# Retention attention into an ELU block on one core: the VectorE side of the ELU, the last output tile and the last weight piece

## The chip, the cores and the metric

The kernel runs on one core of a Trainium2 chip. A core has TensorE (PE in the profile, with its weight loads as PEld), VectorE (DVE), ScalarE (ACT), GpSimd (POOL) and SyncE (SP, which here only issues DMAs). PE writes its results to PSUM, of which the kernel uses eight banks of 512 fp32 columns on 128 partitions; here DVE and ACT read and write PSUM and SBUF, and POOL works on SBUF. The metric is the device time of one execution in microseconds, the median of several runs.

## The reference

```python
scores = scale * np.matmul(q, k.transpose(0, 1, 3, 2))      # q, k, v: 8 batches, 8 heads, 576 positions, 64 wide
Dmat = np.where(rel >= 0, gamma[:, None, None] ** rel, 0.0) # rel = row - column, gamma per head
attn = np.matmul(scores * Dmat, v)
x = attn.transpose(0, 2, 1, 3).reshape(4608, 512)
h = x @ w_in                                                # w_in 512 x 2048
g = np.where(h > 0.0, h, np.exp(np.minimum(h, 0.0)) - 1.0)  # ELU
return g @ w_out                                            # w_out 2048 x 512, fp32
```

The decay `gamma ** (row - column)` splits into a factor for the row and one for the column, so that it can be put on q and k before the product. It is a linear attention with a decaying state.

## The kernel before, in words

The attention is cut into 40 units, five for each batch. Units 0 to 3 of a batch hold 256 positions and four heads each (0 and 1 the first 256 positions, 2 and 3 the next); the fifth, the tail (u = 4, 9, 14, ...), holds the last 64 positions for all heads. For a unit, q, k and v are loaded (step `ld`, on SP's queue), cast to bf16 with the decay factors (`ca`, on POOL, DVE or ACT), transposed (by PE with `tr` and a copy `tc` for units 0 to 7, by a DMA transpose `dt` on SP's queue from unit 8 on), and then PE makes the scores (`sc`), DVE multiplies them with the causal mask (`mk`, L469), PE makes the inner product with v (`va`), the part from the state (`in`) and the state's update (`st`); DVE adds up the state (`pm`, `pe`), DVE or POOL put it in block-diagonal form (`dm`, `de`), and ACT or DVE copy the result to the bf16 tile `xt` (`ou`, L215).

The tokens then go through the two products in nine groups of 512. `f` is the first product for one of the 16 slices of 128 hidden columns (four matmuls of 512 columns, tile `ph`, a PSUM bank). Groups 0 and 1 are cut in two token segments, 256 and 256, 320 and 192, so that the first segment can begin before the second is there. The ELU takes three steps for each `f`: `ex` (L621, ACT: e = exp(ph), fp32 in SBUF), `re` (the side), `el` (the join, DVE, bf16 tile `g`). The side has two forms. On ACT (L627) it is relu(ph) written back over ph in PSUM, and the join is min(e - 1, ph) (L640). On DVE (L631) it is em = min(e - 1, e), a bf16 tile in SBUF made from e alone, and the join is min(max(ph, 0), em) (L642). `a` is a quarter of the second product for 128 tokens (four matmuls of 512 columns, L207, tile `pm`), `y` its copy to SBUF (L215, ACT or DVE), `so` its store (L661, on POOL's queue, for the last four tiles on SP's).

The weights come in four pieces of w_in (`wi.0` to `wi.3`) and four of w_out (`wo.0` to `wo.3`), 512 KB each, on POOL's queue (L295). Quarter m of `a` needs `wo.m` alone.

What each engine does, and in which order, is written out in the string `PLAN` (1559 steps, L23 to L155): the steps are issued in that order, and each engine keeps it for its own. A step with `>` has a gate: `ld.10.q>wo.3` doesn't issue its load until the piece wo.3 has landed, and everything behind it in SP's queue waits too. `wm.8.x1` is eight matmuls on zeros that are thrown away; they keep PE at work while the first loads arrive. PSUM is shared out by bank: h0, h1, h2 and pm, x0 and x1 go round among `f`, `a`, transposes and the attention's results, and the scores have two banks.

The step order around the change, before: POOL's queue issues wi.1, then wi.0, wi.2, wi.3, wo.0, wo.1, wo.2; units 5 and 6 have their k loaded ahead of the weights, all other loads from unit 4 on are behind gates; wo.3 is issued after POOL's cast `ca.5.q.p`. At the end the tiles 8.1, 8.2 and 8.3 of the last group are finished first, and 8.0 last: `a.8.0.3`, then `y.8.0.v` and `so.8.0.y` for 128 tokens by 512 columns.

Of the kernel before, what the change touches and what calls it, by code (L numbers as in the profile page):

```python
# [9 lines left out]
FP32 = mybir.dt.float32  # L10
# [13 lines left out]
ld.1.k ld.0.q wm.8.x1 ld.0.v k0 ld.2.q ld.3.q.1 ld.0.k ca.1.k.p ld.3.v.1 wm.3.h0 ld.1.q ca.0.q.v ld.3.q.0 wm.8.h2  # L24
ld.3.k.1 ld.3.k.0 ld.1.v ld.2.k ca.2.q.p tr.1.k.x0 ld.3.v.0 tr.0.q.x1 tc.1.k.v wm.3.h1 ld.2.v ca.0.k.v wm.6.x0 ld.5.k
ca.0.v.v ld.6.k tc.0.q.v ca.1.q.v wm.2.h2 tr.0.k.h0 st.0 tc.0.k.v ca.3.q.v.1 ca.3.k.p.0 sc.0 pm.0 tr.2.q.x0 pe.0
dm.0.p mk.0 tr.1.q.h2 wm.7.h1 ca.1.v.p tc.1.q.s wi.1 tc.2.q.v ca.2.k.v ca.3.q.p.0 va.0 ca.3.k.v.1 st.1 sc.1 pm.1
tr.3.1.h1 pe.1 in.0 dm.1.p mk.1 tr.3.0.pm ou.0.1.s tr.2.k.h0 wi.0 tc.2.k.s wm.1.x1 ou.0.0.v wi.2 tc.3.0.s in.1
tc.3.1.v sc.2 ca.2.v.s va.1 ca.3.v.v.0 de.0.p wm.2.h1 mk.2 ca.3.v.s.1 ou.1.1.s wi.3 ou.1.0.s st.3.0 st.2 wo.0 pm.2
sc.3.1 st.3.1 sc.3.0 wm.3.x1 mk.3.1 dm.2.p wo.1 mk.3.0 va.2 in.2 pm.3 wo.2 pe.2 ou.2.0.s dm.3.v va.3.0  # L30
f.0.4.0.256.2.h2 ou.2.1.s de.1.v k1 va.3.1 in.3.0 in.3.1 f.0.0.0.256.2.pm ou.3.0.v.0 ou.3.1.s.1 ou.3.1.v.0 ex.0.4.0
ou.3.0.v.1 pe.3 f.0.6.256.256.2.x1 re.0.4.0.s de.3.p ex.0.0.0 el.0.4.0 f.0.6.0.256.2.x0 ex.0.6.256 f.0.11.0.512.1.h2
re.0.6.256.v ex.0.6.0 el.0.6.256 re.0.6.0.s f.0.8.0.512.1.h0 ex.0.11.0 ca.6.k.v f.0.10.0.512.1.h1 re.0.11.0.s el.0.6.0
ex.0.8.0 f.0.4.256.256.2.x1 el.0.11.0 ex.0.10.0 re.0.8.0.v f.0.2.0.256.2.x0 re.0.0.0.s ex.0.4.256 el.0.8.0
f.0.13.0.512.1.h2 ex.0.2.0 el.0.0.0 re.0.4.256.s f.0.0.256.256.2.h0 re.0.10.0.s el.0.4.256 re.0.2.0.s
# [123 lines left out]
def kernel(  # L159
# [9 lines left out]
    nc = tc.nc  # L169
# [543 lines left out]
```

## Time and profile before

| | |
|---|---|
| median of 5 runs | 316.09 us (315.61 to 317.82) |
| the profiled execution | 315.61 us, span 313.9 us, so 1.71 us lie outside the span |
| granted PE clock | 1.00 |
| PE, DVE, ACT, POOL busy | 302.6, 229.6, 174.3, 132.7 us |
| HBM read, written | 36.70 MB, 9.44 MB |
| ELU sides on ACT, on DVE | 110, 42 |

The profile is of one execution. A busy PE includes the fill of its pipeline, so the gaps that it shows are real ones, and some small waits are hidden within busy time. Where durations are given for an operation, they are of one instruction. Idle time of an engine is listed with what ended it.

### The profile page before, as it was taken

To read this page: it belongs to the slowest core of one execution; us is meant where nothing else is said; L and a number is where in the kernel's file an instruction comes from. 1 tells how busy PE (TensorE), PEld (TensorE's weight loads), DVE (VectorE), ACT (ScalarE), POOL (GpSimd) and SP (SyncE) were. 2 spreads that over 40 slices of the span, in tenths; PEclk is the share of its full clock that TensorE was granted. 3 is DMA by queue.
4 is the path that set the end of the run, shared out by engine and by line. 5 is a ranking of instruction groups with operands and counts; after the bars stand their busy time and mean duration, and the time that the engine had idled before them with its cause. 6 is when DMAs were issued, how large, how long until landed. Compare 5 with 4: busy or idle time off the path is not lost.

```text
span 313.9 us, 7897 instructions
## 1 busy us (share of the span) xinstructions
PE 302.6 (96%) x3143; PEld 155.6 (50%) x3143; DVE 229.6 (73%) x435; ACT 174.3 (56%) x365; POOL 132.7 (42%) x196
## 2 busy tenths in 40 slices
PE   8999998999999989999998999999999999999995
PEld 3557554567555444444544454445444444444442
DVE  2888867997879957759899787898966585653512
ACT  2049946587258577563865556645636576745200
POOL 5480174666778455282695469522002120000100
PEclk9999999999999999999999999999999999999999
DMA  7999999999998999999699996121200010001034
GB/s 203 267 190 200 190 245 225 243 229 225 261 219 203 231 272 243 225 246 258 176 241 277 268 173 134 34 73 63 52 21 33 37 67 2 0 25 44 0 115 153
DMA packets 101140, 49.92 MB, mean 159 GB/s; under 512 B 45296, under 2 KB 98544, under 8 KB 101104
## 3 DMA queue, kind: packets, MB, share of 16 engines
q1 hardware_dynamic: 94320, 36.84, 53.8%
q0 software_dynamic: 6784, 12.59, 16.3%
q8 instruction: 24, 0.39, 0.5%
q14 instruction: 12, 0.10, 0.1%
HBM read 36.70 MB, written 9.44 MB: 147 GB/s over the span
## 4 chain that ended last, share of the span: by engine, by line
PE 76%; DMA 10%; DVE 7%; POOL 2%; SPq 2%; issue 1%; ACT 1%; ACTq 0%; DVEq 0%
PE pm L207 35%; PE ph L207 31%; DMA w_out<-in_moe_w_out_dram 7%; PE x L207 5%; PE warm L207 3%; DVE em L631 2%; PE sc L207 2%; DMA rvt<-in_v_dram 2%; DMA rqk<-in_q_dram 1%; DVE pt L469 1%; SPq L383 1%; DVE g L640 1%; POOL w_in L295 1%; DVE g L642 1%; ACT e L621 1%
## 5 line engine op out<-in xcount | busy, mean ns | idle before, releaser
L207 PE MATMUL ph<-xt,w_in 128*128 128x512 bf16 (+3 forms) x672 | 142.0, 349 | 2.7 <-DVE g L642 1.6
L207 PE MATMUL pm<-w_out,g 128*128 128x512 bf16 x576 | 142.9, 379 | 0.8 <-DMA w_out<-in_moe_w_out_dram 0.8
L621 ACT ACTIVATE e<-ph 128x512 f32<-128x512 f32 (+2 forms) x152 | 86.8, 575 | 78.3 <-PE ph L207 74.2
L207 PEld LDWEIGHTS <-w_in 128*128 128x128 bf16 x672 | 63.1, 98 | 60.8 <-issue 3.4
L640 DVE SCALAR_TENSOR_TENSOR g<-e,ph 128x512 bf16<-128x512 f32 (+3 forms) x123 | 71.0, 596 | 27.5 <-ACT ph L627 26.2
L207 PEld LDWEIGHTS <-g 128*128 128x128 bf16 x576 | 54.6, 98 | 62.0 <-issue 1.4
L627 ACT ACTIVATE ph<-ph 128x512 f32<-128x512 f32 (+2 forms) x110 | 62.4, 573 | 0.0
L661 POOL DMA_DIRECT2D out_dram<-ot x32 | 18.2, 570 | 85.6 <-DVE ot L215 54.6
L631 DVE SCALAR_TENSOR_TENSOR em<-e 128x512 bf16<-128x512 f32 (+2 forms) x42 | 37.1, 885 | 14.4 <-ACT e L621 14.1
L469 DVE TENSOR_TENSOR pt<-sc,mask 128x1024 bf16<-128x1024 f32 x31 | 37.7, 1215 | 0.7 <-PE sc L207 0.6
L367 POOL TENSOR_TENSOR qkn<-rqk,gq 128x512 bf16<-128x512 f32 (+1 forms) x26 | 28.0, 1075 | 14.5 <-DMA rqk<-in_q_dram 11.7
L367 POOL TENSOR_TENSOR qkn<-rqk,gk 128x512 bf16<-128x512 f32 (+1 forms) x24 | 25.2, 1050 | 13.6 <-DMA rqk<-in_k_dram 10.1
L215 ACT CAST xt<-x 128x256 bf16<-128x256 f32 (+1 forms) x59 | 19.9, 388 | 17.6 <-PE x L207 15.9
L642 DVE SCALAR_TENSOR_TENSOR g<-ph,em 128x512 bf16<-128x512 f32 (+3 forms) x45 | 28.1, 631 | 1.1
L566 POOL TENSOR_TENSOR s_mid<-mid,diag 128x256 bf16<-128x256 f32 x26 | 17.6, 678 | 19.3 <-DVE mid L557 10.9
L215 ACT COPY ot<-pm 128x512 f32<-128x512 f32 x22 | 12.9, 589 | 18.2 <-PE pm L207 18.1
L566 POOL TENSOR_TENSOR s_end<-end,diag 128x256 bf16<-128x256 f32 x25 | 15.8, 638 | 14.9 <-DVE end L563 14.9
L215 DVE COPY ot<-pm 128x512 f32<-128x512 f32 x14 | 9.5, 687 | 13.1 <-PE pm L207 13.1
L215 DVE CAST xt<-x 128x256 bf16<-128x256 f32 (+1 forms) x31 | 11.6, 387 | 7.6 <-PE x L207 5.0
L362 POOL TENSOR_TENSOR qkt<-rqt,gq 128x256 bf16<-128x256 f32 x13 | 9.0, 701 | 16.0 <-DMA rqt<-in_q_dram 13.2
L215 POOL CAST vn<-rv 128x512 bf16<-128x512 f32 x18 | 11.2, 624 | 9.8 <-PE x L207 6.2
L207 PE MATMUL warm<-zero 128*128 128x512 bf16 x43 | 13.1, 459 | 1.3 <-DVE zero L220 1.3
(64 smaller groups left out, 185.0 us busy)
## 6 DMA issues: line engine op xcount, KB each, us to landing
out_dram<-ot POOLq DMA_DIRECT2D x32, 256.0 KB, 3.2
rqk<-in_k_dram SPq DMA_DIRECT2D x31, 256.0 KB, 5.2
rqk<-in_q_dram SPq DMA_DIRECT2D x31, 256.0 KB, 4.9
rv<-in_v_dram SPq DMA_DIRECT2D x31, 256.0 KB, 4.3
w_in<-in_moe_w_in_dram POOLq DMA_DIRECT2D x4, 512.0 KB, 7.0
w_out<-in_moe_w_out_dram POOLq DMA_DIRECT2D x4, 512.0 KB, 11.9
rqt<-in_k_dram SPq DMA_DIRECT2D x8, 128.0 KB, 4.8
rqt<-in_q_dram SPq DMA_DIRECT2D x8, 128.0 KB, 4.1
```

The costliest lines, as they stand in the source:

```text
L207: return pin(nc.tensor.matmul(*a, **kw))
L215: return pin(nc.scalar.copy(dst, src) if eng == "s" else engines[eng].tensor_copy(dst, src))
L362: return pin(engines[eng].tensor_tensor(dst[:, hs], src[:, hs], g, ALU.mult))
L367: return pin(engines[eng].tensor_tensor(to, x, g, ALU.mult))
L469: return pin(nc.vector.tensor_tensor(ptt[u].rearrange("p h i n -> p i h n"), sc.rearrange("p i (h n) -> p i h n", h=2), m.unsqueeze(1).to_ ...
L566: return pin(engines[eng].tensor_tensor(dst.rearrange("p h (j d) -> p h j d", j=2), src.unsqueeze(2).to_broadcast([P, 2, 2, D]), diag.unsq ...
L621: return pin(nc.scalar.activation(e[:, : n * nf], ph[:, : n * nf], AF.Exp))
L627: return pin(nc.scalar.activation(ph[:, : n * nf], ph[:, : n * nf], AF.Relu))
L631: return pin(nc.vector.scalar_tensor_tensor(em[:, : n * nf], e, -1.0, e, ALU.add, ALU.min))
L640: last = pin(nc.vector.scalar_tensor_tensor(dst, more[0][:, c], -1.0, ph[:, c], ALU.add, ALU.min))
L642: last = pin(nc.vector.scalar_tensor_tensor(dst, ph[:, c], 0.0, more[1][:, c], ALU.max, ALU.min))
L661: return pin({"p": nc.gpsimd, "y": nc.sync}[eng].dma_start(out[i0 : i0 + P, :], ots.pop((int(g), int(it)))))
```

## The change

Three edits in the Python, and a new `PLAN`.

1. The side of the ELU on DVE is relu(ph), written back over ph in PSUM, as it was on ACT. The tile em is gone, and there is one form of the join.
2. The output tile 8.0 is made in two halves of 256 columns, each with 16 matmuls into a PSUM bank of its own (h1 and x1), a copy of its own (the first on ACT, the second on DVE) and a store of its own on SP's queue.
3. `wo.3` is issued with the other weight pieces, ahead of the loads that have gates. The pieces go out as wi.1, wi.2, wi.3, wi.0, wo.1, wo.2, wo.0, wo.3. The first load with a gate is `ld.5.q>wo.0`.

The plan is another one throughout (1556 steps, none of its first steps in the old place). It holds the same work of PE but for the halves and the zero matmuls (43 before, 38 after). Which engine does a step changes as follows:

| steps | before | after |
|---|---|---|
| ELU side, ACT / DVE | 110 / 42 | 88 / 64 |
| casts of q and k, POOL / DVE | 63 / 19 | 68 / 14 |
| casts of v, POOL / ACT / DVE | 23 / 12 / 6 | 17 / 23 / 1 |
| block-diagonal states, POOL / DVE | 51 / 13 | 56 / 8 |
| copies to xt, ACT / DVE | 52 / 30 | 48 / 34 |
| copies of transposes, ACT / DVE | 6 / 9 | 7 / 8 |
| copies of output tiles, ACT / DVE | 22 / 14 | 19 and a half tile / 16 and a half tile |

```diff
 PLAN = """
-ld.1.k ld.0.q wm.8.x1 ld.0.v k0 ld.2.q ld.3.q.1 ld.0.k ca.1.k.p ld.3.v.1 wm.3.h0 ld.1.q ca.0.q.v ld.3.q.0 wm.8.h2
-ld.3.k.1 ld.3.k.0 ld.1.v ld.2.k ca.2.q.p tr.1.k.x0 ld.3.v.0 tr.0.q.x1 tc.1.k.v wm.3.h1 ld.2.v ca.0.k.v wm.6.x0 ld.5.k
...
-sc.3.1 st.3.1 sc.3.0 wm.3.x1 mk.3.1 dm.2.p wo.1 mk.3.0 va.2 in.2 pm.3 wo.2 pe.2 ou.2.0.s dm.3.v va.3.0
-f.0.4.0.256.2.h2 ou.2.1.s de.1.v k1 va.3.1 in.3.0 in.3.1 f.0.0.0.256.2.pm ou.3.0.v.0 ou.3.1.s.1 ou.3.1.v.0 ex.0.4.0
...
-f.0.12.0.512.1.pm el.0.10.0 ex.0.13.0 el.0.2.0 f.0.14.0.512.1.h1 re.0.13.0.s ex.0.0.256 el.0.13.0 ld.4.k>wo.1
...
-re.0.2.256.s ld.7.k>wi.3 el.0.12.0 ca.5.v.p ld.4.v>wi.2 a.0.1.1 el.0.2.256 ex.0.15.0 ca.5.q.p re.0.15.0.s a.0.0.2
-ld.7.v>wo.0 ca.6.v.s wo.3 el.0.15.0 tr.4.q.pm ld.9.k>wi.1 tr.5.q.x1 tc.4.q.v a.0.1.2 ca.7.q.p ld.8.q tc.5.q.s
...
-a.8.2.0.h2 a.8.1.3 a.8.2.1 y.8.1.v so.8.1.y a.7.3.3 a.8.2.2 y.7.3.v a.8.3.2 so.7.3.p a.8.2.3 a.8.3.3 y.8.2.v so.8.2.y
-a.8.0.3 y.8.3.s so.8.3.y y.8.0.v so.8.0.y
+ld.0.k ld.0.q wm.7.x1 ld.1.q k0 ld.1.k ld.6.k ld.3.v.0 ca.0.k.p ld.0.v ld.2.k tr.0.k.h1 wm.6.x0 ld.2.q ld.1.v ld.3.q.0
+ld.3.k.0 wm.7.h2 ca.1.k.v ld.2.v ca.1.q.v ld.3.v.1 ca.0.q.v ld.3.k.1 wm.4.h0 ld.3.q.1 tc.0.k.v ca.0.v.p ld.5.k
+tr.0.q.pm tr.1.k.x0 tr.1.q.h0 ca.2.k.v wm.4.h2 tc.0.q.v tr.2.k.x1 ca.2.q.p sc.0 st.0 mk.0 wm.7.h1 ca.1.v.s tc.2.k.s
+ca.3.q.p.0 pm.0 wi.1 tc.1.k.v tr.2.q.pm pe.0 va.0 ca.2.v.s tc.2.q.v ca.3.k.p.0 st.1 tc.1.q.s dm.0.p pm.1 ca.3.v.s.1
+wi.2 pe.1 sc.1 in.0 mk.1 wm.3.h2 dm.1.p ou.0.0.s ou.0.1.s ca.3.k.p.1 st.2 sc.2 ca.3.q.p.1 pm.2 tr.3.0.h0 mk.2 in.1
+wi.3 tc.3.0.s va.1 tr.3.1.pm ca.3.v.s.0 wi.0 ou.1.1.s st.3.1 tc.3.1.v ou.1.0.v sc.3.1 de.0.p st.3.0 sc.3.0 va.2 mk.3.1
+f.0.6.0.256.2.pm dm.2.p pm.3 de.1.p mk.3.0 in.2 ex.0.6.0 dm.3.p pe.2 ou.2.1.v va.3.0 ou.2.0.s wo.1 in.3.0 in.3.1
+ou.3.1.v.0 va.3.1 wo.2 ou.3.0.v.0 f.0.4.0.256.2.h2 ou.3.0.v.1 ou.3.1.v.1 pe.3 ca.5.k.p f.0.4.256.256.2.x1 ex.0.4.0
+re.0.6.0.s k1 re.0.4.0.v f.0.11.0.512.1.x0 ex.0.4.256 wo.0 el.0.4.0 f.0.6.256.256.2.h0 ex.0.11.0 ca.6.k.p el.0.6.0
+f.0.14.0.512.1.h1 ex.0.6.256 re.0.4.256.v de.2.p re.0.11.0.s f.0.10.0.512.1.pm el.0.4.256 ex.0.14.0 de.3.p
+f.0.8.0.512.1.h2 el.0.11.0 wo.3 ex.0.10.0 re.0.6.256.v re.0.14.0.s f.0.2.256.256.2.x1 ex.0.8.0 el.0.14.0 re.0.10.0.s
+el.0.6.256 f.0.0.0.256.2.h1 ex.0.2.256 el.0.10.0 re.0.8.0.s ex.0.0.0 el.0.8.0 f.0.2.0.256.2.pm re.0.0.0.s
+f.0.0.256.256.2.h2 el.0.0.0 ex.0.2.0 tr.6.k.h0 re.0.2.0.v ex.0.0.256 f.0.9.0.512.1.x0 el.0.2.0 re.0.0.256.s
+f.0.15.0.512.1.h1 ex.0.9.0 tc.6.k.v re.0.2.256.v f.0.12.0.512.1.pm el.0.2.256 ld.5.q>wo.0 a.0.0.0.h0 el.0.0.256
+ex.0.15.0 re.0.15.0.s ex.0.12.0 ld.4.k>wo.0 tr.5.k.x1 re.0.9.0.v a.0.1.0.h2 ld.4.q>wi.1 tc.5.k.v ld.6.q>wi.2 el.0.15.0
+f.0.13.0.512.1.x1 ld.5.v>wo.2 el.0.9.0 a.0.1.1 ld.7.k>wo.0 re.0.12.0.v ex.0.13.0 ld.4.v re.0.13.0.v a.0.0.1 ca.5.q.p
+el.0.12.0 a.0.1.2 ld.6.v>wo.3 ca.4.q.v ca.4.k.p ld.7.v>wo.0 a.0.0.2 el.0.13.0 ld.7.q>wi.1 ca.6.q.v tr.5.q.x0 tr.4.q.h1
+ld.8.v>wo.1 tc.5.q.s a.0.1.3 ca.5.v.p ld.9.k>wo.2 tc.4.q.s tr.6.q.pm ld.9.q>wo.2 y.0.1.v st.5 ca.4.v.p ca.7.k.p sc.4
+sc.5 ld.8.q>wo.1 pm.5 a.0.0.3 mk.4 ld.10.k>wi.0 pe.5 mk.5 a.0.3.0.h2 dm.5.p ld.8.k>wi.3 ca.6.v.s ld.10.q>wo.3 y.0.0.s
...
+so.7.2.p a.8.3.2 a.7.3.1 a.8.1.3 a.8.2.2 y.8.1.v so.8.1.y a.8.3.3 a.7.3.2 y.8.3.s a.8.2.3 so.8.3.y a.7.3.3 y.8.2.v
+so.8.2.y b.8.0.0.h1 y.7.3.v so.7.3.p b.8.0.1.x1 yb.8.0.0.s sb.8.0.0.y yb.8.0.1.v sb.8.0.1.y
 """
...
-        ph, n, nf, more = es[int(g), int(ft), int(lo)]
+        ph, n, nf, e = es[int(g), int(ft), int(lo)]
         if eng == "s":
             return pin(nc.scalar.activation(ph[:, : n * nf], ph[:, : n * nf], AF.Relu))
-        em = epool.tile([P, TG], BF16, name="em", tag="em")
-        more.append(em)
-        e = more[0][:, : n * nf]
-        return pin(nc.vector.scalar_tensor_tensor(em[:, : n * nf], e, -1.0, e, ALU.add, ALU.min))
+        return pin(nc.vector.tensor_scalar_max(ph[:, : n * nf], ph[:, : n * nf], 0.0))
...
-            if len(more) == 1:
-                last = pin(nc.vector.scalar_tensor_tensor(dst, more[0][:, c], -1.0, ph[:, c], ALU.add, ALU.min))
-            else:
-                last = pin(nc.vector.scalar_tensor_tensor(dst, ph[:, c], 0.0, more[1][:, c], ALU.max, ALU.min))
+            last = pin(nc.vector.scalar_tensor_tensor(dst, e[:, c], -1.0, ph[:, c], ALU.add, ALU.min))
...
+    def ffn2_columns(g, it, c, tag):
+        g, it, c = int(g), int(it), int(c)
+        accs[g, it, c] = bank(tag, "pm")
+        for ft in range(NFT):
+            last = mm(accs[g, it, c][:, : DM // 2], gts[g, ft][:, it * P : (it + 1) * P],
+                      w_sb["o"][ft // 4][:, ft % 4, c * DM // 2 : (c + 1) * DM // 2],
+                      start=(ft == 0), stop=(ft == NFT - 1))
+        return last
+
+    def out_y_columns(g, it, c, eng):
+        g, it, c = int(g), int(it), int(c)
+        ots[g, it, c] = opool.tile([P, DM // 2], FP32, name="oc", tag="oc", bufs=2)
+        return copy(eng, ots[g, it, c], accs[g, it, c][:, : DM // 2])
+
+    def store_columns(g, it, c, eng):
+        g, it, c = int(g), int(it), int(c)
+        i0 = g * TG + it * P
+        return pin({"p": nc.gpsimd, "y": nc.sync}[eng].dma_start(
+            out[i0 : i0 + P, c * DM // 2 : (c + 1) * DM // 2], ots.pop((g, it, c))))
```

## The prediction

> **What bounds the kernel now.** I read the page's busy times first, then the busy time in stretches of 10 us, then the chain of work that ended last, and for the operations that the change touches the groups by shape and the timeline.
>
> ```profile
> PE 302.6 (96%) x3143; PEld 155.6 (50%) x3143; DVE 229.6 (73%) x435; ACT 174.3 (56%) x365; POOL 132.7 (42%) x196
> PEclk9999999999999999999999999999999999999999
> ```
>
> PE is busy for 302.64 of 313.9 us at a clock of 1.00, so the change can only move the 11.26 us in which PE stands still, or PE's work in the start. Where they lie (columns: stretch, length, then PE, PEld, DVE, ACT, POOL busy, clock, DMA share, GB/s):
>
> ```profile
> 0.00:10.00 10.00, 8.75 (x34) 3.71 (x35) 3.50 (x24) 2.01 (x4) 4.70 (x19) 1.00 0.83 222
> 10.00:20.00 10.00, 8.92 (x205) 5.33 (x204) 9.18 (x19) 3.59 (x8) 7.56 (x11) 1.00 1.12 223
> ...
> 40.00:50.00 10.00, 9.18 (x151) 5.10 (x149) 6.67 (x15) 4.48 (x11) 5.57 (x7) 1.00 1.18 246
> 50.00:60.00 10.00, 9.31 (x139) 5.48 (x138) 8.76 (x15) 6.50 (x17) 6.32 (x9) 1.00 0.95 211
> 60.00:70.00 10.00, 9.58 (x180) 6.33 (x179) 9.78 (x23) 7.42 (x22) 7.12 (x9) 1.00 1.19 242
> ...
> 110.00:120.00 10.00, 8.55 (x99) 4.25 (x97) 6.19 (x11) 8.52 (x20) 5.47 (x7) 1.00 1.18 277
> ...
> 160.00:170.00 10.00, 8.42 (x85) 3.95 (x84) 9.93 (x12) 4.85 (x11) 8.36 (x12) 1.00 1.15 250
> ```
>
> Start 2.33 us; then 0.82 + 0.69 + 0.42 + 1.45 + 1.58, with 0.04 in 20-30 and 0.21 in 200-210: 5.21 us; and 3.73 us after PE's last matmul ends at 310.17. The chain says what the 0.82 us at 48 us waits for:
>
> ```profile
> 21.66 14.57 DMA w_out<-in_moe_w_out_dram
> 36.25 4.19 DMA rqk<-in_q_dram
> 40.52 0.99 POOL qkn L367
> 41.51 7.17 DMA w_out<-in_moe_w_out_dram
> 48.72 1.89 PE pm L207 x8
> ```
>
> The seventh weight piece lands at 36.23, a gated load of q behind it at 40.4, POOL casts it, and only then issues wo.3, for which PE waits until 48.72. For 160-170, the timeline:
>
> ```profile
> 162.99 0.62 POOL L215 CAST vn<-rv 128x512 bf16<-128x512 f32 x1
> 163.26 3.90 DVE L631 SCALAR_TENSOR_TENSOR em<-e 128x512 bf16<-128x512 f32 x1
> 163.57 1.05 POOL L367 TENSOR_TENSOR qkn<-rqk,gk 128x512 bf16<-128x512 f32 x1
> 164.57 1.05 POOL L367 TENSOR_TENSOR qkn<-rqk,gq 128x512 bf16<-128x512 f32 x1
> 165.57 1.04 POOL L367 TENSOR_TENSOR qkn<-rqk,gk 128x512 bf16<-128x512 f32 x1
> ...
> 168.02 1.02 PE L207 MATMUL ph<-xt,w_in 128*128 128x512 bf16 x4 [1.20 <-DVE g L642]
> ```
>
> One em took 3.90 us beside four POOL casts in a row, and ended 0.55 us after the last of them; its join came late, and PE had no free bank. The prices, by shape:
>
> ```profile
> L631 DVE SCALAR_TENSOR_TENSOR em<-e 128x512 bf16<-128x512 f32 x37 | 32.7, 884 | 14.4 <-ACT e L621 14.1
> L642 DVE SCALAR_TENSOR_TENSOR g<-ph,em 128x512 bf16<-128x512 f32 x36 | 24.6, 687 | 0.9
> L215 DVE COPY ot<-pm 128x512 f32<-128x512 f32 x14 | 9.5, 687 | 13.1 <-PE pm L207 13.1
> L627 ACT ACTIVATE ph<-ph 128x512 f32<-128x512 f32 x91 | 54.1, 599 | 0.0
> ```
>
> **The change, part by part.** The sum is made against the profiled execution: span 313.9, time 315.61, so 1.71 outside. It is the fastest of five; the median is 0.48 higher, which I add at the end.
>
> *The ELU side.* Removed: 42 em, 37.2 us of DVE. Added: 64 relus in PSUM, which the trace doesn't show on DVE. From below the nearest is the DVE copy out of PSUM in bf16 (0.42 for 512), from above the mean em with its waits (0.88). I take 0.687, the DVE copy of the same 512 fp32 columns out of PSUM, because only the place of the result differs, and on ACT that place costs nothing (in place 0.599, exp into SBUF 0.598). The joins keep their price (0.681 with e, 0.687 with em). 57 x 0.687, 4 of 320 columns x 0.475 and 3 of 384 x 0.54 are 42.7 us. With what else moves on DVE (10 casts x 0.68 less, 5 states x 0.42 less, one transpose copy x 0.42 less, 4 copies to xt x 0.44 and 2.5 output copies x 0.69 more) its total changes by 42.7 - 37.2 - 6.8 - 2.1 - 0.4 + 1.8 + 1.7 = -0.3 us: DVE stays near 229 us. ACT loses 22 relus and gains 11 casts (-13.0 + 6.8) and falls below 170. Both are work beside PE. On the path is only the waiting: the 1.58 us of 160-170 and the 0.21 us of 200-210, where the chain also runs through an em (1.49 us at 203.29), go: -1.8. Neither wait is added to: the relu waits for exp as em did, with the same join queued behind it on DVE.
>
> The Trainium skill (SBUF - State Buffer, section "SBUF: two separate sides") says that a DVE instruction with two SBUF inputs and a GpSimd instruction take turns on a port pair, each holding it whole. The 3.90 us em agrees. By that rule the 15 casts left on DVE can still be held up, the relus can't, and the sum would be the same -1.8. Against the change speaks VectorE: DVE Perf Modes, section on the TRN2 errata: 120 cycles of fixed cost for a PSUM source against 58 for SBUF. By that the sum would lose an estimated 64 x 62 cycles / 0.96 GHz = 4.1 us of DVE work; the rows 0.687 (PSUM) and 0.692 (median em) show no such difference.
>
> *The last tile.* PE does the same: a 256-column matmul in the first product takes 7.8 us / 64 = 122 ns, a 512-column one 119.2 / 480 = 248. The last copy is 256 columns wide: 0.41 as the join of that width, for 0.69: -0.28. The store is 128 KB instead of 256: the DMA moves up to 410 GB/s there, so -0.32 us of the 2.0 us from issue to landing; bounds 0 (all of it fixed) and -0.65. The first half's copy and store and the extra issue on SP lie beside the second half's 16 matmuls (about 1.9 us). Sum -0.6, between -0.3 and -0.9.
>
> *Weights and the start.* Loads: 17 before the weights in both plans, about 0.9 us each 256 KB. Walking the new order with the rows' durations: POOL casts q of unit 3 at 12.3 and issues wi.1 at 13.05 (13.57 before); mask 1 runs 15.1-16.3, mask 2 16.75-17.95, mask 3 from 19.0, each held by the two score banks; the first `f` starts at 19.4 (21.81 before), but the second must wait for unit 3's states, which are now all on POOL behind wi.3 and wi.0: 22.2, against 23.26. So the start gains 1.05. Then 13 more `f` of 0.866 and a transpose bring PE to `a.0.0.0` at 34.6. That needs wo.0, now the seventh piece, and the seventh landed at 36.2; 0.2 earlier with wi.1: a new wait of 1.4. In its place before, PE was at this step at 35.77. The start's gain is gone: +0.2.
>
> Behind that gate stands all of SP's queue: units 4 to 8 start loading at 36.0, not 33.42, and wo.3's 512 KB run ahead of them (2.5 us at the 205 GB/s of 20-40 us). v of unit 6 lands near 46.5, ACT casts it (0.62), and `st.6`, which PE reaches at 46.4, waits some 0.7; the 0.82 us for wo.3 are gone. Going on, PE begins group 1 at 52.1 (52.22 before): -0.1 for all of it. k of unit 8 has 3968 KB ahead and with it: 55.4 at 205 GB/s, 53.3 at 230 (the page shows 225 and 245 there). Cast 1.04, transpose 1.3 and 4.1 to land: 61.8 or 59.7, and PE wants its scores near 59: between 0 and 2.8; I take +0.6. Early part +0.5, bounds -1.9 (the start's gain and the 0.82 kept) and +4.
>
> *The order elsewhere.* The 1.45 us at 112 are v of unit 19: issued at 104.58, landed at 110.28, cast on ACT. Between its load and its use lie 6.0 us of PE work in the old plan, 20.7 in the new one: gone. New waits of the kind have to be reckoned with; the loads nearest to their use in the new plan are v of units 5 and 6 (5.0, 4.8 us, counted above), 9 (5.6) and 36 (5.4, when the DMA is nearly idle); and DVE has up to 11.7 us of work for 10 us of PE around 50-60 (11.2 before). I take +1.0 for them, between 0 and 4.
>
> Sum: -1.8 - 0.6 + 0.5 - 1.45 + 1.0 = -2.35. Span 311.55, run 313.26, median 313.7.
>
> **The rivals.** *No change:* the plan trades waits for waits; gaps after the start come to about 5 us again. For it: DVE's total is the same, and the start's gain meets the weights. Against: em's hold-ups (9 us over undisturbed ones: 37 x 0.192 and 3 x 0.64) can't return. Only the tail stays: 315.5.
>
> *Starved early, about no change or slower:* the 2.6 us of the gate and the 2.5 us of wo.3 reach PE whole, in 45-62 us: 5.1 - 0.1 instead of +0.5. -2.35 + 4.5 = +2.1: 318.2. It is slower once the early part comes to more than 4.5 us. For it: v of units 5 and 6 stand within 5 us of their use. Against: four quarters `a.0.2` can fill, and in the old plan SP stood at its gate from 45.0 to 48.7 and doesn't now.
>
> *DVE becomes the bound, slower:* the relu costs the upper price: 64 x 0.19 = 12.2 us more on DVE, which is over 0.78 busy in most stretches up to 230 us; half of it reaches PE: -2.35 + 6.1: 319.8. It decides from 0.81 us a relu (64 x 0.124 / 2 = 3.95). For it: no row shows this operation. Against: the DVE copy at 0.687.
>
> **How the numbers follow.** About 0.5%, 1.6 us, is what a measurement of this kernel can tell from no change. Forecast 0.47, all of it faster; no change 0.20, same; starved 0.17, half same and half slower; DVE bound 0.16, slower. So faster 0.47, same 0.28, slower 0.25. The forecast's own range is 311.0 to 314.5. For 8 in 10 the lower end is the early part at -1.9 with the tail's -0.9: 310.9; the upper end goes between the two slower cases, 319.0.
>
> **What would show it.** Right: no em, relus near 0.69 us with hardly any spread; PE full in 160-170 and 110-120; a wait for w_out at `a.0.0.0` near 36 us and none at 48; 3.1 us after the last matmul. Wrong: relus above 0.8, or PE waiting for x, sc or DMA rows between 45 and 70 by more than 4 us; a start that gains 2 us and keeps it would make it better than forecast.

## The result and the profile after

The changed kernel takes 315.32 us (median; 312.63 to 318.05) beside 316.46 us for the kernel before in the same comparison: a ratio of 0.9983, with a 95% interval from 0.9967 to 0.9999. That is 0.5 us, and less than the 0.5% that this kernel's measurement can tell from no change. Forecast were 313.7 us and a gain of 0.74%. This ratio and those below leave out disturbed executions, which took over 1.5% more than the fastest of their kernel (24 of the 80 of before, 2 of the 43 of the changed kernel); that is why it isn't the ratio of the two medians.

The profiled execution took 313.78 us with a span of 312.1, 1.8 us under the profiled one of before, near the forecast's -2.35. It flatters the kernel: it is 1.5 us under its own median, where before's was 0.5 us under the median of its first five runs.

The page of the changed kernel, busy times (us, share of the span, instructions):

```profile
PE 300.9 (96%) x3154; PEld 156.4 (50%) x3154; DVE 226.5 (73%) x449; ACT 167.3 (54%) x348; POOL 131.2 (42%) x200
```

DVE is 3 us lower than before (229.6) and ACT 7 us (174.3). The busy time in stretches of 10 us (stretch, length, then PE, PEld, DVE, ACT, POOL busy, clock, DMA share, GB/s):

```profile
0.00:10.00 10.00, 7.59 (x35) 3.04 (x36) 3.56 (x24) 2.01 (x4) 3.75 (x19) 1.00 0.83 219
...
40.00:50.00 10.00, 9.95 (x157) 5.69 (x154) 7.63 (x16) 3.48 (x8) 6.36 (x9) 1.00 1.26 244
...
80.00:90.00 10.00, 7.67 (x135) 4.43 (x133) 4.26 (x12) 3.71 (x9) 7.47 (x11) 1.00 1.19 241
...
110.00:120.00 10.00, 10.00 (x81) 4.74 (x79) 8.24 (x17) 6.61 (x14) 5.96 (x7) 1.00 1.05 242
...
160.00:170.00 10.00, 10.00 (x140) 4.96 (x138) 7.24 (x14) 5.64 (x14) 8.43 (x12) 1.00 0.95 202
```

The waits of before at 48, 112 and 165 us are gone. But in all PE stands still for 11.1 us, and it was 11.3 before: new are 2.33 us at 80-90, 1.2 us more in 0-10 (2.41 for 1.25) and 0.9 us more in 20-40. What makes this span shorter is PE's work, 300.9 us for 302.6: the zero matmuls take 10.0 us and not 12.6. So waits were traded for waits, and the 1.8 us of this profile are not those of the forecast's sum. The groups by shape:

```profile
L635 DVE SCALAR_TENSOR_TENSOR g<-e,ph 128x512 bf16<-128x512 f32 x120 | 80.3, 682 | 17.3 <-ACT ph L626 15.5
L627 DVE TENSOR_SCALAR ph<-ph 128x512 f32<-128x512 f32 x57 | 39.7, 696 | 21.1 <-ACT e L620 20.7
```

A relu takes 0.696 us; the longest of all 64 took 0.700. The timeline shows the new wait:

```profile
78.41 1.26 SPq L383 DMA_TRANSPOSE qkT<-qkt  x1
...
82.05 1.14 ACT L215 CAST vn<-rv 128x512 bf16<-128x512 f32 x2 [0.88 <-DMA rv<-in_v_dram]
...
82.71 0.32 PE L207 MATMUL x<-vn,qkn 64*64 64x64 bf16 x16 [0.64 <-ACT vn L215]
...
84.95 0.26 PE L207 MATMUL x<-qkT 64*64 64x64 bf16 x8 [1.69 <-DMA qkT<-qkt]
```

v of unit 13 was issued at 77.07 and lands about 82, when PE already wants it; the transposing DMA of unit 14, issued at 78.41, is there at 84.9. In before these were issued at 73.1 and 75.0, with their uses at the same place (82 us).

### The profile page after: what moved, and what is told of

Its sections match the earlier page's. It is cut to its first block, busy times and chain, and to the rows that moved or that the text cites. A ratio compares the mean times of both kernels' runs of the same rounds, so it can differ in the third digit from the quotient of the medians.

```text
span 312.1 us, 7915 instructions
## 1 busy us (share of the span) xinstructions
PE 300.9 (96%) x3154; PEld 156.4 (50%) x3154; DVE 226.5 (73%) x449; ACT 167.3 (54%) x348; POOL 131.2 (42%) x200
## 4 chain that ended last, share of the span: by engine, by line
PE 77%; DMA 14%; POOL 4%; SPq 3%; issue 1%; DVE 1%; POOLq 0%; DVEq 0%
PE pm L207 36%; PE ph L207 33%; PE x L207 5%; DMA w_out<-in_moe_w_out_dram 4%; DMA qkT<-qkn 3%; SPq L332 2%; PE sc L207 2%; DMA qkT<-qkt 2%; DMA out_dram<-ot 2%; DMA rqk<-in_q_dram 2%; DMA rqt<-in_q_dram 1%; POOL qkn L367 1%; POOL w_in L295 1%; POOL s_mid L566 1%; POOL w_out L295 0%
## 5 line engine op out<-in xcount | busy, mean ns | idle before, releaser
L207 PE MATMUL pm<-w_out,g 128*128 128x512 bf16 (+1 forms) x592 | 143.3, 373 | 0.1
L635 DVE SCALAR_TENSOR_TENSOR g<-e,ph 128x512 bf16<-128x512 f32 (+3 forms) x168 | 97.8, 605 | 18.8 <-ACT ph L626 16.5
L627 DVE TENSOR_SCALAR ph<-ph 128x512 f32<-128x512 f32 (+2 forms) x64 | 43.2, 676 | 22.0 <-ACT e L620 21.6
L626 ACT ACTIVATE ph<-ph 128x512 f32<-128x512 f32 (+2 forms) x88 | 49.5, 570 | 0.0
L367 POOL TENSOR_TENSOR qkn<-rqk,gk 128x512 bf16<-128x512 f32 (+1 forms) x27 | 27.3, 1013 | 16.3 <-DMA rqk<-in_k_dram 15.2
L215 DVE COPY ot<-pm 128x512 f32<-128x512 f32 x16 | 11.0, 689 | 15.1 <-PE pm L207 12.6
L215 ACT COPY ot<-pm 128x512 f32<-128x512 f32 x19 | 11.1, 586 | 16.3 <-PE pm L207 16.1
L215 ACT CAST vn<-rv 128x512 bf16<-128x512 f32 (+1 forms) x18 | 10.5, 593 | 15.0 <-DMA rv<-in_v_dram 15.0
L215 POOL CAST vn<-rv 128x512 bf16<-128x512 f32 x14 | 8.6, 613 | 18.2 <-DMA rv<-in_v_dram 18.2
L207 PE MATMUL sc<-qkT 64*64 64x128 bf16 x512 | 13.1, 219 | 1.6 <-DMA qkT<-qkn 0.7
L207 PEld LDWEIGHTS <-qkT 64*64 64x64 bf16 x576 | 9.6, 107 | 8.1 <-issue 4.3
```

The lines of the kernel that those rows point to most:

```text
L207: return pin(nc.tensor.matmul(*a, **kw))
L215: return pin(nc.scalar.copy(dst, src) if eng == "s" else engines[eng].tensor_copy(dst, src))
L367: return pin(engines[eng].tensor_tensor(to, x, g, ALU.mult))
L626: return pin(nc.scalar.activation(ph[:, : n * nf], ph[:, : n * nf], AF.Relu))
L627: return pin(nc.vector.tensor_scalar_max(ph[:, : n * nf], ph[:, : n * nf], 0.0))
L635: last = pin(nc.vector.scalar_tensor_tensor(dst, e[:, c], -1.0, ph[:, c], ALU.add, ALU.min))
```

## Experiments

In what follows the *old order* is the step list of before, the *new order* that of the changed kernel. All ratios are to the kernel before, run beside them.

### The three edits, one by one, in the old order

**Relu alone.**

```diff
-        em = epool.tile([P, TG], BF16, name="em", tag="em")
-        more.append(em)
-        e = more[0][:, : n * nf]
-        return pin(nc.vector.scalar_tensor_tensor(em[:, : n * nf], e, -1.0, e, ALU.add, ALU.min))
+        return pin(nc.vector.tensor_scalar_max(ph[:, : n * nf], ph[:, : n * nf], 0.0))
```

> The kernel before with one edit: on VectorE the ELU side is the relu in place in PSUM, at the 42 places where em stood; order, weights and last tile as before. Theory 'given back' (the gains that were forecast are there in every execution, and new waits of the new order took them away): the 1.58 us of idle PE in 160-170 and the 0.21 us of 200-210 are gone, relu near 0.69 us each, ratio 0.994 (-1.8 us). Theory 'one execution' (the hold-up of em read in one profile stands in few executions, so that its removal is worth little): ratio 0.997 to 1.001, even if the gap at 160-170 is gone from this profile. Theory 'no better than em': relus with waits near 0.8 us or more, PE idle elsewhere, ratio 1.002 or more.

Measured: 312.58 us, ratio 0.9896 (0.9857 to 0.9934): 3.3 us less, between 2.1 and 4.5. The gain that was forecast is there and is larger.

**Halves alone.**

```diff
-a.8.0.0.x0 ... a.8.0.1 ... a.8.0.2 ... a.8.2.0.h2 ... a.8.2.1 ... a.8.2.2 ... a.8.0.3 ... y.8.0.v so.8.0.y
+a.8.2.0.x0 ... a.8.2.1 ... a.8.2.2 ... b.8.0.0.h1 b.8.0.1.h2 yb.8.0.0.s sb.8.0.0.y yb.8.0.1.v sb.8.0.1.y
```

> The kernel before with the last output tile alone in column halves: tile 2 of group 8 takes the last tile's early places and its bank, and the last tile is computed at the end as two halves on two banks, copied by ACT and VectorE, with a store each. Up to about 295 us this is the program of before, so its profile is a second execution of that part. Tail: 3.1 us after the last matmul against 3.73, ratio 0.998 (-0.6 us); if the half's store takes as long as the whole one, 0.999. 'Given back' expects the idle PE of before at 110-120 (1.45 us) and at 160-170 (1.58 us) here again within 0.3 us each; 'one execution' expects at least one of them under half of that.

Measured: 316.04 us, ratio 1.0005 (0.9966 to 1.0043). After the last matmul 3.1 us are left (it ends at 311.27 of 314.4), as expected, but 0.6 us can't be told at this interval. Up to there this is the program of before, so the question whether em's hold-up was of one execution is answered. The timeline of this run:

```profile
164.32 3.90 DVE L631 SCALAR_TENSOR_TENSOR em<-e 128x512 bf16<-128x512 f32 x1
...
164.62 1.05 POOL L367 TENSOR_TENSOR qkn<-rqk,gk 128x512 bf16<-128x512 f32 x1
...
165.62 1.04 POOL L367 TENSOR_TENSOR qkn<-rqk,gq 128x512 bf16<-128x512 f32 x1
...
166.62 1.03 POOL L367 TENSOR_TENSOR qkn<-rqk,gk 128x512 bf16<-128x512 f32 x1
```

and its stretch:

```profile
160.00:170.00 10.00, 8.44 (x84) 3.88 (x83) 9.83 (x13) 4.78 (x11) 8.98 (x13) 1.00 1.18 249
```

The longest em took 3.905, 3.896 and 3.898 us in three profiles of this order, with 1.56 us of idle PE here beside 1.58 before. The theory "one execution" falls for em. The other gap that this run was to show again, at 110-120, came to 0.91 us and not to 1.45 within 0.3: that one does change between executions. With the relu in its place (the run above), in the same order and beside the same POOL casts, the timeline and the stretch are:

```profile
162.85 0.69 DVE L628 TENSOR_SCALAR ph<-ph 128x512 f32<-128x512 f32 x1
...
163.04 1.05 POOL L367 TENSOR_TENSOR qkn<-rqk,gk 128x512 bf16<-128x512 f32 x1
```

```profile
160.00:170.00 10.00, 9.94 (x139) 5.21 (x138) 7.41 (x13) 5.93 (x13) 7.84 (x13) 1.00 1.27 236
```

**Last weight piece alone.**

```diff
-... va.2 in.2 pm.3 wo.2 pe.2 ... ca.6.v.s wo.3 el.0.15.0 ...
+... va.2 in.2 pm.3 wo.2 wo.3 pe.2 ... ca.6.v.s el.0.15.0 ...
```

> The kernel before with the last weight piece alone moved: issued right behind the third piece of its kind, ahead of the gated loads. The 0.82 us wait for it at 48 us is gone; the gated loads of units 4 to 8 start up to 2.5 us later (512 KB at 205 GB/s). By the forecast's terms the loads have room and the ratio is 0.997 to 1.000; if they are starved, PE waits 1 to 3 us more between 45 and 65 us and the ratio is 1.003 to 1.010. 'One execution' expects no difference beyond 0.2% either way.

Measured: 317.04 us, ratio 0.9995 (0.9954 to 1.0037): nothing that can be told. In its profile, which is of its longest execution (321.02 us), no wait for w_out is left, but PE waits 1.92 us at 41-44 for POOL's casts of units 4 and 5. In the run with all three edits, the next one, it is 1.82 us at the same place: the wait moved.

**All three.** The three diffs above together.

> The kernel before, in its own order, with all three edits: relu in PSUM, last tile in halves, last weight piece early. 'Given back' expects the sum of the three, 0.989 to 0.993, and so clearly less time than the changed kernel (0.998). 'One execution' expects 0.996 to 0.999, level with the changed kernel.

Measured: 312.96 us, ratio 0.9907 (0.9876 to 0.9939). So the edits in the old order keep what the relu gives, and the changed kernel, at 0.9983, has the same three edits and 2.4 us more (by the two intervals 1.3 to 3.5). What takes them back lies in its order or in what it puts on which engine.

### What the new order costs

**Em back in the new order.** The diff of the relu, reversed, in the changed kernel, with the join of before.

> The changed kernel with em back in SBUF, and its join, at the 64 places of the relu; order, weights and halves of the changed kernel. If the gain of the relu (ratio 0.990 alone in the old order) is also in the new order, and the new order's own waits took it back ('given back'), em here costs at least as much as there, being 64 and not 42 instructions: ratio to the kernel before 1.006 to 1.020, VectorE busy 10 us more than the 226.5 of the changed kernel, and single ems above 2 us. If the new order had made the relu worthless (a rival: its 64 places are ones at which em would not be held up), the ratio stays at 0.996 to 1.000.

Measured: 316.20 us, ratio 1.0011 (0.9979 to 1.0043), less than was expected. VectorE is busy 238.1 us, three ems took 2.4 to 2.7 us, and PE waits 4.9 us for joins. Compared with the changed kernel that is +0.3%: here the relu is worth about 0.9 us, and by the two intervals anything from -0.2 to 2.0. The waits for joins (0.7 us in the changed kernel) are not simply added: the wait of 1.7 us for the transposing DMA at 83 isn't in this profile.

**The last tile whole in the new order.**

```diff
-b.8.0.0.h1 y.7.3.v so.7.3.p b.8.0.1.x1 yb.8.0.0.s sb.8.0.0.y yb.8.0.1.v sb.8.0.1.y
+a.8.0.0.h1 a.8.0.1 y.7.3.v so.7.3.p a.8.0.2 a.8.0.3 y.8.0.v so.8.0.y
```

> The changed kernel with the last output tile whole again: four quarters on one bank, one copy by VectorE, one store. Until about 305 us this is the program of the changed kernel, so its profile is a second execution of that. Tail 3.7 us after the last matmul and not 3.1; ratio to the kernel before 0.998 to 1.000, +0.2% on the changed kernel's 0.998. If the idle PE of the new order is of its own making, it is here again within 0.5 us each: 2.4 us in 0-10 and 2.3 us in 80-90.

Measured: 314.91 us, ratio 0.9989 (0.9961 to 1.0018). Its profile is a second execution of the new order, with 2.15 us of idle PE in 0-10 and 1.95 in 80-90: these belong to the order, though their size doesn't: 0-10 has 1.6 to 1.9 us in the profiles of the four runs that follow.

**The gap at 80-90 filled with ready work, or its transfers moved forward, or both.**

```diff
-sc.13 ... st.13 va.12 sc.14 a.1.2.1 ... a.1.1.2 ... a.1.2.2 ... a.1.1.3
+sc.13 a.1.2.1 a.1.1.2 ... st.13 va.12 a.1.2.2 sc.14 ... a.1.1.3
```

> The changed kernel with three steps of PE moved: the quarters a.1.2.1 and a.1.1.2 go ahead of the state of unit 13, and a.1.2.2 ahead of the scores of unit 14, so that 2.6 us of ready work lie where PE waited 2.3 us between 81 and 85 us for a cast of v and for a transposing DMA. 'Given back' expects that gap gone and its time kept: ratio 0.990 to 0.993 to the kernel before, against 0.998 of the changed one. If the gap was of that one execution, or if the wait only moves behind the quarters: 0.996 to 0.999.

```diff
-ld.12.v in.10 ... dt.13 ld.16.v ... ld.15.k ... ca.12.v.p ca.14.v.s ld.13.v ld.15.q ... dm.11.p ... ca.14.k.p ... dt.14
+ld.12.v ld.13.v in.10 ... dt.13 ... ca.14.k.p dt.14 ld.16.v ld.15.k ca.12.v.p ca.14.v.s ld.15.q ... dm.11.p ...
```

> The changed kernel with the work for units 13 and 14 moved forward on its queues, and PE's order as it was: v of unit 13 is loaded right behind v of unit 12 (some 5 us earlier), k of unit 14 is cast ahead of v of unit 12 on POOL, and its transposing DMA goes ahead of three loads (78.4 before, about 76 expected). If the 2.3 us of idle PE at 80-90 are the lateness of these two transfers, at most 0.6 us are left there and the ratio is 0.989 to 0.993. If they only push the next transfer (unit 15's, or v of unit 12) as late: a gap of over 1.2 us stays between 75 and 100 and the ratio is 0.995 to 0.999.

> The changed kernel with both repairs of 80-90 us: the quarters of the second product ahead of the waits, and the transfers for units 13 and 14 moved forward (each alone 0.994). If the late transfers are the cause of what is lost there, the idle PE of 70-100 is 1.5 us or less and the ratio 0.989 to 0.992. If each of the two had only moved the wait and gained by something else, 0.993 to 0.996.

Measured: 0.9936 (0.9905 to 0.9967), 0.9936 (0.9909 to 0.9963) and, with both, 0.9960 (0.9929 to 0.9992). Each of the first two gains 1.5 us on the changed kernel, but not by the mechanism that was expected: in their profiles the idle PE of 80-90 is still there (2.05 and 2.85 us; 0.16 us of each is a matmul that the trace lacks). In the first, VectorE's list has the state's sum before the masks, so delaying the state delayed the masks and PE waited for them from 85.8; in the second, the loads that were passed came later in their turn (q of unit 15 landed at 85.75 and not at 82.84), POOL got to its cast of v of unit 15 only at 87.97, and PE waited 2.64 us for that. The two don't add up. That the late transfers cost some of the 2.4 us is likely from these runs; how much, and where the gain went, stays open.

**The relus put back on their engines.** Of the 152 ELU sides, 110 were on ACT and 42 on VectorE before; the change moved 37 from ACT to VectorE and 15 back. In the new order each relu goes to the engine that the old order had for that tile; in the old order (with the relu in PSUM) each goes where the new order has it. The last letter of a step is its engine, v for VectorE and s for ACT. One of the 52 steps in the new order, in the old one the other way round:

```diff
-re.0.13.0.v
+re.0.13.0.s
```

> The changed kernel with each relu on the engine on which the old order had the ELU side of that tile (37 go back from VectorE to ACT, 15 the other way; VectorE has 42 of 152), relu in PSUM, all else as changed. If the 22 relus more on VectorE take back part of the gain, VectorE is 10 us less busy than 226.5 and the ratio is 0.992 to 0.995 (against 0.998). If the loss is in the transfers of the new order alone, 0.997 to 1.000; if ACT, which was freed by them, now comes late, 1.001 or more.

> The old order with the relu in PSUM on VectorE at the 64 tiles at which the changed kernel has it, and on ACT at the others; nothing else. Against 0.990 of the same with 42 of them. If VectorE is near its bound, VectorE is 10 us busier (230) and the ratio is 0.994 to 0.999. If VectorE has room, 0.988 to 0.992.

Measured: in the new order 313.97 us, ratio 0.9923 (0.9887 to 0.9958), against 0.9983 with 64 on VectorE. In the old order 314.83 us, ratio 0.9973 (0.9946 to 1.0000), against 0.9896 with 42. With 22 relus more on VectorE, which is 13.8 and 15.1 us busier for it, the kernel takes 0.6% more in the one (by the two intervals 0.2 to 1.0) and 0.8% in the other (0.3 to 1.2): 1.9 and 2.4 us, about what was missing. Since 52 sides change engine for these 22, the runs don't tell the number of the relus from the choice of the tiles. PE's waits in the old order, with 42 relus on VectorE (who waits for whom; us, times, longest):

```profile
PE x L207 <- ACT xt L215: 1.7, 1, 1.7
...
PE ph L207 <- DVE g L637: 0.2, 1, 0.2
```

and with 64:

```profile
PE ph L207 <- DVE g L637: 2.2, 5, 0.9
...
PE x L207 <- DVE g L637: 0.2, 1, 0.2
```

The longest of the five, in the timeline of the latter:

```profile
30.89 0.69 DVE L628 TENSOR_SCALAR ph<-ph 128x512 f32<-128x512 f32 x1
...
32.29 0.69 DVE L628 TENSOR_SCALAR ph<-ph 128x512 f32<-128x512 f32 x1
...
32.89 1.34 DVE L637 SCALAR_TENSOR_TENSOR g<-e,ph 128x512 bf16<-128x512 f32 x3
...
33.62 1.68 PE L207 MATMUL ph<-xt,w_in 128*128 128x512 bf16 x7 [0.86 <-DVE g L637]
```

and the same place with 42, where VectorE has no relu in 30-34 and is itself idle before its joins:

```profile
31.57 2.66 DVE L637 SCALAR_TENSOR_TENSOR g<-e,ph 128x256 bf16<-128x256 f32 x6 [0.57 <-ACT ph L627]
32.97 1.41 PEld L207 LDWEIGHTS <-w_in 128*128 128x128 bf16 x8 [0.66 <-DVE g L637]
32.97 1.90 PE L207 MATMUL ph<-xt,w_in 128*128 128x512 bf16 x8 [0.17 <-DVE g L637]
```

The joins stand behind the two relus and end late, the bank of `ph` stays taken, and PE has nowhere to put the next tile. The second longest has another cause:

```profile
100.45 2.16 DVE L367 TENSOR_TENSOR qkn<-rqk,gq 128x512 bf16<-128x512 f32 x1
...
102.53 0.68 DVE L637 SCALAR_TENSOR_TENSOR g<-e,ph 128x512 bf16<-128x512 f32 x1
...
103.13 1.21 DVE L469 TENSOR_TENSOR pt<-sc,mask 128x1024 bf16<-128x1024 f32 x1
...
103.26 1.02 PE L207 MATMUL ph<-xt,w_in 128*128 128x512 bf16 x4 [0.65 <-DVE g L637]
```

This join stands behind a cast of q on VectorE that took 2.16 us, beside casts on POOL, where it takes 0.68 us in the run with 42. It isn't a matter of the relus: in the last run of this document, with 27 of them, the same cast took 2.17 us and PE waited 0.65 us again. So some 1.4 of the 2.4 us can be followed to joins in this one profile; the rest isn't traced.

In the new order the same move is less visible in PE's waits (0.7 us for joins with 64, 1.0 with 42). There the transposing DMAs of units 8 to 16 go out 1.2 to 2.5 us earlier with 42 than in the changed kernel's profile (unit 14's at 77.1 and not 78.4; 0.3 to 2.1 us earlier than in that of the kernel with the whole tile), and the wait for the one falls from 1.7 us to 0.2. But about 0.5 us of lead stands already ahead of the first relu (a run of matmuls into `ph` that begins at 22.7 us in both of these profiles begins at 22.2 with 42), and PE's wait for ACT's cast of v of unit 13 rises from 0.6 to 1.1 us: in all 80-90 has 1.54 us of idle PE for 2.33. VectorE is busy 8.99 us of 70-80 in the one and 7.68 in the other. That the placement is the cause is shown by the times in both orders; that it works through the transposes in the new one is one reading of one profile each, and not shown.

**Fewer still.**

In the old order with the relu in PSUM, 15 more steps go from VectorE to ACT, as this one:

```diff
-re.1.14.0.v
+re.1.14.0.s
```

> The old order with the relu in PSUM, on VectorE at the 27 tiles that both kernels have there and on ACT at the other 125: the third point beside 42 (0.990) and 64 (0.997) relus on VectorE. VectorE is about 210 us busy, ACT 183. If every relu on VectorE costs PE, 0.985 to 0.988; if 42 was already where joins come in time, 0.988 to 0.992; if ACT's exps now come late, 0.993 or more.

Measured: 314.18 us, ratio 0.9912 (0.9874 to 0.9949), level with 42. VectorE is busy 211.8 us, ACT 180.8. So in the old order the step from 42 relus to 27, from 220 to 212 us of VectorE's work, is worth nothing that can be told, and the one from 64 to 42, from 235 to 220 us, is worth 0.8%. Beside each other the runs make no single line (em, with its hold-ups, takes more time for the same load), so no bound for VectorE's load follows from them:

| order | ELU side on VectorE | VectorE busy, us | ratio |
|---|---|---|---|
| new | 64 em | 238.1 | 1.0011 |
| old | 64 relu | 235.1 | 0.9973 |
| old | 42 em (before) | 229.6 | 1 |
| new | 64 relu (the change) | 226.5 | 0.9983 |
| old | 42 relu, all three edits | 221.4 | 0.9907 |
| old | 42 relu | 220.0 | 0.9896 |
| old | 42 em with one input (below) | 218.3 | 0.9966 |
| new | 42 relu | 212.7 | 0.9923 |
| old | 27 relu | 211.8 | 0.9912 |

### What holds em up

```diff
-        return pin(nc.vector.scalar_tensor_tensor(em[:, : n * nf], e, -1.0, e, ALU.add, ALU.min))
+        return pin(nc.vector.tensor_scalar_add(em[:, : n * nf], e, -1.0))
```

> The kernel before with em computed from e once: em = e - 1 as one input and a constant (the minimum of e - 1 and e is e - 1), where before both inputs of the instruction were the same SBUF tile e. Same 42 places, same e, same join, same result tile in SBUF. If the hold-ups come with an instruction of VectorE that has two SBUF inputs beside GpSimd's, ems are at 0.69 us or below with none above 1.0, the 1.56 us of idle PE at 160-170 are gone, and the ratio is that of the relu, 0.988 to 0.993: then it was not PSUM that gained, but one SBUF input less. If any VectorE instruction that works from SBUF to SBUF is held up, single ems above 2 us stay and the ratio is 0.997 to 1.001.

Measured: 314.90 us, ratio 0.9966 (0.9930 to 1.0003), between em and the relu, and by the interval not quite clear of em. Most are faster, 0.427 us (median) against 0.692, but the hold-up stays, beside the same three POOL casts:

```profile
163.29 3.63 DVE L631 TENSOR_SCALAR em<-e 128x512 bf16<-128x512 f32 x1
...
163.59 1.05 POOL L367 TENSOR_TENSOR qkn<-rqk,gk 128x512 bf16<-128x512 f32 x1
...
167.77 0.59 PE L207 MATMUL ph<-xt,w_in 128*128 128x512 bf16 x2 [0.93 <-DVE g L642]
```

So a hold-up doesn't need the second SBUF input. It may come with any work from SBUF to SBUF, or with the faster mode that 0.427 us points to; these runs don't tell the two apart. This run takes as little of VectorE's time as the relu (218.3 and 220.0 us) and is 0.7% behind it (by the two intervals 0.2 to 1.2); the difference left in it is the place of the operands, and with it these hold-ups. That they are what the 0.7% are is argued and not shown: its profile has 1.1 us of waits for joins, beside 0.2 with the relu alone, and its longest wait is one of 2.5 us for w_out at 48 us, which is 0.7 to 0.9 us in the profiles of before, of the relu alone and of the halves alone. The Trainium skill (SBUF - State Buffer, section "SBUF: two separate sides") names both kinds of VectorE instruction for its lock against GpSimd, those with two SBUF inputs and those in a mode that uses both ports. The prediction had taken only the first; the one-input em and the relus, none above 0.701 us in any profile, agree with the page as a whole. A hold-up is not one-sided either: POOL, too, is busy longer beside em than beside the relu, 132.7 us for 130.4 in the old order and 137.4 for 131.2 in the new one.

### Versions that beat both

The old order with the three edits, and three quarters moved:

```diff
-a.0.0.2 ... tr.4.q.pm ... tr.5.q.x1 ... a.0.1.2 ... st.5 sc.4 sc.5 ... a.0.3.0.h1 ... va.19 ... a.2.0.2
+a.0.0.2 ... a.0.1.2 tr.4.q.pm ... a.0.3.0.h1 tr.5.q.x1 ... st.5 sc.4 sc.5 ... a.2.0.2 va.19 ...
```

and then the load of v of unit 19 as well:

```diff
-ld.20.v ld.24.q ld.29.q ... dt.20 ld.19.v
+ld.20.v ld.19.v ld.24.q ld.29.q ... dt.20
```

> The old order with all three edits (0.991 in the run before), and three quarters of the second product moved ahead of waits: a.0.1.2 and a.0.3.0 ahead of the two transposes at 41 us (1.8 us of idle PE in the profile of that run) and a.2.0.2 ahead of the values of unit 19 at 110 us (0.8 to 1.8 us). If these waits stand in most executions: 1.5 to 2.5 us less, ratio 0.983 to 0.987. If they move behind the quarters or were of single executions: 0.989 to 0.992.

> The old order with all three edits and the three moved quarters (0.989 in the run before), and v of unit 19 loaded right behind v of unit 20, ahead of two loads of q and a transposing DMA, some 3 us earlier. The idle PE at 110-120 (0.56 us in the run before) goes: ratio 0.985 to 0.988; if that transposing DMA comes late for it, 0.989 to 0.991.

Measured: 312.27 us, 0.9886 (0.9852 to 0.9920), and 312.17 us, 0.9873 (0.9830 to 0.9917). The second has the lowest ratio of this study, 1.1% under the changed kernel. The three quarters were to give 1.5 to 2.5 us on the run with all three edits (0.9907) and gave 0.7, which can't be told from nothing. Without halves and early weight piece (relu, `a.2.0.2` and `ld.19.v` alone), and with only 27 relus on VectorE:

> The old order with the relu in PSUM, one quarter (a.2.0.2) ahead of the values of unit 19, and v of unit 19 loaded some 3 us earlier; the last tile whole and the last weight piece late, as before. If halves and weight piece add nothing (1.0005 and 0.9995 alone), the ratio is that of the run with everything, 0.985 to 0.989; if they are worth their forecast 0.6 and 0.5 us, 0.989 to 0.991.

> The fastest version so far (old order, three edits, three quarters and a load moved: 0.987) with the relu on VectorE at 27 tiles only. By the same three cases 0.982 to 0.985, 0.985 to 0.989, or 0.990 or more.

Measured: 0.9887 (0.9840 to 0.9933) and 0.9896 (0.9845 to 0.9947). These four and the relu alone can't be told apart: nearly all of the gain is the relu, one for one.

## Why the prediction was wrong

Forecast was -0.74%, measured -0.17%. By steps:

- **The relu's price: right.** 0.687 us was taken from the copy out of PSUM; measured 0.696, never held up.
- **"The 1.58 us of 160-170 and the 0.21 us of 200-210 go: -1.8": right in kind, too small.** Alone the exchange gives -3.3 us (-2.1 to -4.5). It was sized by the two gaps of one profile. PE's waits for joins were 1.8, 3.0 and 1.8 us in three profiles with em, and 0.2 with the relu alone (0.2 to 0.7 in the five profiles of the old order with 42 relus). The 3.0 hold a wait of 1.3 us that no em made: its join stands behind a cast on VectorE that was held up beside POOL's work, as the prediction had said of the 15 casts left there.

```profile
57.88 2.15 DVE L367 TENSOR_TENSOR qkn<-rqk,gk 128x512 bf16<-128x512 f32 x1
...
59.95 0.47 DVE L640 SCALAR_TENSOR_TENSOR g<-e,ph 128x320 bf16<-128x320 f32 x1
...
60.47 0.42 PE L207 MATMUL x<-pt,vn 64*64 64x128 bf16 x16 [1.30 <-DVE g L640]
```

  So em's share is 1.6 to 1.8 us in each of the three, as forecast; where the rest of the 3.3 us comes from, these traces don't show.

- **"Both are work beside PE ... Neither wait is added to": this failed.** The working had VectorE's total right ("near 229 us", measured 226.5), and read from it that only em's waits count. But the exchange itself takes 9.6 us off VectorE (229.6 to 220.0), and the 22 relus from ACT put 13.8 to 15.1 us back on it. Costed at nothing, they cost +1.9 us (new order) to +2.4 us (old order), so the ELU side as a whole brought -0.9 to -1.4 us and not the -3.3 of the exchange. ACT, from which they came, had 174 us of work and needed no relief: with 180.8 us of it no loss can be told. The cover that was named, the wait for exp, isn't where the joins are late: they stand behind other VectorE work, relus in one place and a cast that was held up in another.
- **The last tile: right in the trace** (3.1 us after the last matmul, 3.7 before) and below what the timing can tell: alone 1.0005, where -0.2% were forecast.
- **The early part: right in outline.** The first `f` began at 20.1 (forecast 19.4, before 21.8), `a.0.0.0` at 36.2 (36.0), where PE stood idle for only 0.1 us ahead of the weight piece and not for 1.4, since it came later itself; no wait is left at 48 us, group 1 began at 51.5 (52.1), and the scores of unit 8 waited 0.5 (0.6). The last piece's move alone: 0.9995.
- **"I take +1.0 for new waits": too small in the profile,** where 80-90 alone has 2.33 us. The places were sought by PE's work between a load and its use in the step list. v of unit 13 has some 7 us by that count, but SP reached its load late, and it was issued 5 us before its use. A load's distance has to be counted from when its queue gets to it.
- **"+0.48 to the median": not a constant.** The changed kernel's profile lies 1.5 us under its median, that of the relu alone 1.0 us above.

By terms, from the runs: relu one for one -1.0%, 22 relus more on VectorE +0.6 to +0.8%, halves and weight piece 0.0 (each to 0.4%), the rest of the new order +0.2% (0.9923 against 0.9907, to 0.5%). That comes to -0.2 to 0.0%, for -0.17%. That the forecast of the profiled span came so near (-2.35, and -1.8 in the one profile) is luck: the idle time of PE that it added up stayed the same. The rival "no change" had named a reason that holds, waits traded for waits with VectorE's total the same, and gave 315.5 us; the one with VectorE as the bound had a part of the mechanism, with a wrong cause (the price of a relu, where the runs show where and how many they are).

## What to carry to other kernels

Here the exchange of an instruction that was held up for one that never was, at the same undisturbed price, was worth more than the waits that one profile showed, and over half of it was spent again when other work moved to that engine: compare the engine's total, and where its joins stand in its list, not the price of one. Try such an edit alone in the old order before a new order is planned around it. And read two profiles of the same program before a gap is sized, since gaps of over a microsecond come and go between executions (the 1.3 us above, and 1.45 or 0.91 us at 110-120).

## What the runs showed of the hardware

A pause of PE cost more than itself. Busy time in stretches of 1 us of the changed kernel with the last tile whole (the clock is the third number from the end):

```profile
82.00:83.00 1.00, 0.02 (x3) 0.00 (x0) 0.00 (x0) 0.00 (x0) 0.77 (x1) 1.00 1.11 265
83.00:84.00 1.00, 0.26 (x8) 0.26 (x10) 0.00 (x0) 0.00 (x0) 0.00 (x0) 1.00 1.06 292
84.00:85.00 1.00, 0.77 (x2) 0.30 (x3) 0.85 (x3) 0.66 (x2) 0.55 (x1) 0.50 1.18 328
...
86.00:87.00 1.00, 1.00 (x4) 0.38 (x3) 1.00 (x5) 0.45 (x1) 1.00 (x3) 0.50 2.51 202
87.00:88.00 1.00, 1.00 (x5) 0.38 (x4) 0.88 (x3) 0.00 (x0) 1.00 (x2) 0.79 0.32 66
88.00:89.00 1.00, 1.00 (x6) 0.36 (x4) 0.00 (x0) 0.00 (x0) 1.00 (x2) 1.00 1.14 369
```

After 1.95 us of idle PE within 3.5 us the granted clock was 0.50 for about 3.4 us, and the 512-column matmuls of the second product followed each other every 0.427 us there, and every 0.216 after it: some 1.7 us of PE's work lost, by an estimate from these two. Over the profiles, eight places have 1.89 us or more of idle PE within 3.5 us. The clock fell at six of them: 1.89 (quarters moved), 1.94 (both repairs), 1.95 (above), 1.92 and 2.56 (weight piece alone), 2.52 (em with one input). It held at 2.33 (the changed kernel) and 2.64 (transfers moved). Where the idle time was 1.82 us or less it never fell (all counted from 4 to 300 us). The Trainium skill (TensorE: Matmul & The Clock Gate, section "HAM oscillation - how this bites in real kernels") sets the bound at idle gaps above about 3.4 us; here about 1.9 us of idle was enough at most places. So the price of a gap near 2 us changes from one execution to the next, which no single profile shows: 1.95 and 2.33 are the same place of the same step list.

The clock is also a rival for the difference between the kernels, and the granted clock is on record for the executions of the changed kernel, of the experiments and of before beside these. It was 0.996 or less, as a mean, in 34 of 124 executions of the kernel before (318.8 us on average; the others 315.8), in 18 of 44 of the changed kernel (316.0; 314.9) and in none of the 6 with the relu alone. Among the executions above that the order stays: before 315.8 us, the changed kernel 314.9, the old order with 64 relus 314.8, the new order with 42 relus 313.4, the relu alone 312.4. So the clock adds to what a wait costs, but it isn't what took the gain back.
